# Attention with a gate beside it: first weights in halves, a regrouped lead, another bank for V's last tile, and a tile finished by VectorE

## The chip, the cores and the metric

One NeuronCore of one Trainium2 chip. The metric is the device time of one execution, in microseconds (us). TensorE (PE) multiplies matrices into eight PSUM banks of 128 x 512 f32; VectorE (DVE) and ScalarE (ACT) read PSUM, GpSimd (POOL) does not touch it here; SyncE (SP), ScalarE and GpSimd issue transfers. Every engine works through its own instructions in the order in which the program wrote them, and semaphores hold an instruction back until what it reads is there and what it overwrites has been used.

## The reference

x is 2048 x 512. The result mixes two branches, g a + (1 - g) b, with g = sigmoid(x . gate_w):

```python
qkv = (x @ wqkv).reshape(B, S, 3, 32, 16)            # 32 heads of 16
p = softmax(einsum("bhqd,bhkd->bhqk", q, k) * 16 ** -0.5)
a = einsum("bhqk,bhkd->bhqd", p, v) ... @ wo
r = x @ w_r;  idx = argsort(-r)[:2]                  # two routed tokens
y = (silu(x[idx] @ w_gate) * (x[idx] @ w_up)) @ w_down * sigmoid(r[idx])
b = x with y added in the rows idx
```

## The kernel before, in words

**Numbers in two pieces.** Projections are made of f32 split into a high and a low f32r piece (`split`, L68: ScalarE writes the high piece, VectorE or GpSimd the difference). A product then has three terms: high by high, high by low, low by high.

**Attention.** Heads are worked in pairs, a pair in two halves of 1024 queries: a unit. There are 32 units of 16 steps, one step for each tile of 128 keys. `s_piece` (L664) makes 128 keys x 512 queries of scores transposed (S) for one head and has ScalarE take the exponential into P (L674); the two heads lie in different rows of the array (partitions 0 and 64). `av_mm` (L689) multiplies P by V into the bank av over a unit's 16 steps; V carries a column of ones, which gives the sums. The exponentials need each query's largest score first. That is a second product of Q and K, 48 rows deep, reduced by VectorE (`m_piece`, L578): 64 products a unit, `EL`. When a unit's are there, `m_unit` (L640) combines them, and `m_rows` (L654) puts the negated maxima as two more rows below Q by eight small transfers, so that S comes out already lowered.

**The banks.** Tags of the PSUM pool: st (three banks, S and, at the beginning, projections and V), mxa (two banks as one tile), mxb, fl and av (one each). A tile waits until what was in its bank has been read.

**The order.** It is written out by hand (`manual_schedule`). First TensorE is kept busy with ten matmuls of zeros (L231). `load_w(0)` (L111) asks for the first projection weights, K's part first, and with them the first block of x: two of its four pieces by ScalarE's queue, all else by SyncE's. Projections of pair group 0 follow (`proj0`), evicted into split tiles that are stored to HBM and, for the first pair, copied straight into Kx and Qx.

Then comes the lead (L1000): `LEAD` = 21 steps, in which `m_lead` (L612) makes the maxima of the first unit and a part of the second ahead of any S, and `parts_next` mixes in the parts of `lead_parts` (L305): four parts of the last Q projection and 64 parts of V, a part being three matmuls (`v_part`, L294); four parts make one tile of V in an st bank. A lead step makes two pairs of maxima products, one pair into mxa and one into two of mxb, fl and av in turn, has three reductions of them, and then three parts (four in the first step). `end_step(s)` runs what is due after step s: `products` and `sums` (GpSimd multiplies x by w_r and by gate_w, ScalarE sums the rows), loads, `split_w(1)` after step -5, and after step -1 `r_row` (L342), which transposes the 2048 router scores on TensorE.

The main loop (L1009) follows `ORDER`, four steps a pass: s is an S piece, m a maxima product, A the P V of an earlier step, f a piece of other work (later projections, the routed feed-forward, the output projection). The first two A's have no P V to do yet; they take the parts of V that the lead has left over, two each.

**The tail** (L789) is what the last unit leaves: normalise its result and multiply it by wo for tiles 12 to 15 (L836), with the output products of tiles 9, 10 and 11 put between (`late_wo`). A tile of the output is finished either by `finish` (L560: one VectorE instruction reads PSUM, scales by g and adds to acc) or by `acc_add` (L474: ScalarE scales into a buffer, GpSimd adds it to acc). `store` (L564) writes a finished tile by SyncE's queue; tile 15 goes out in two halves by ScalarE's.

Of the kernel before, what the change touches and what calls it, by code (L numbers as in the profile page):

```python
# [21 lines left out]
KT = S // 128  # L22
VW = DH + 1
LEAD = 21
STEPS = UNITS * KT
EL = 64
# [10 lines left out]
def gated_mix(ctx: ExitStack, tc: tile.TileContext, xT, x, wqkv, wo, w_rg, w_gate, w_up, w_down,  # L37
# [18 lines left out]
    def mxa_tile():  # L56
        return psum.tile([128, 2, 512], F32, tag="mxa", name="mxa", bufs=1)
# [4 lines left out]
    def av_tile():  # L62
        return psum.tile([128, 512], F32, tag="av", name="av", bufs=1)
# [48 lines left out]
    def load_w(g):  # L112
        ws = ring.tile([128, 2, 4, 128], F32, tag="w", name="ws", bufs=3)
        W[g] = ws
        for i in (1, 0):
            if g == 0 and i == 0:
                load_x(0)
            nc.sync.dma_start(ws[:, i], ap(wqkv, (2 * g + i) * 128 * D, [[D, 128], [128, 4], [1, 128]]))

    def split_w(g, parts=(1, 0)):  # L120
# [14 lines left out]
    def load_x(nb):  # L135
        xst.append(ring.tile([128, 4, 512], F32, tag="xs" if nb < 2 else "P", name="xs", bufs=2 if nb < 2 else 3))
        for c in range(4):
            eng = nc.scalar if nb == 0 and c % 2 == 0 else nc.sync
            eng.dma_start(xst[nb][:, c], ap(xT, (nb * 4 + c) * 128 * 512, [[512, 128], [1, 512]]))

    def split_x(nb):
# [86 lines left out]
    warm = ring.tile([128, 512], mybir.dt.bfloat16, tag="o", name="warm", bufs=6)  # L228
    nc.vector.memset(warm, 0.0)
    wps = st_tile()  # L230
    for _ in range(10):  # L231
        nc.tensor.matmul(wps, warm[:, :128], warm, start=True, stop=True)
    load_w(0)
    for nb in range(1, 4):
# [58 lines left out]

    def v_part(t, c):  # L294
        if c == 0:
            VP[t] = st_tile()
        ps = VP[t]
        nb, tt = divmod(t, 4)
        sl = slice(tt * 128, tt * 128 + 128)
        for n, (a, b) in enumerate(((xh, wv[1]), (xl, wv[1]), (xh, wv[2]))):  # L300
            nc.tensor.matmul(ps, a[nb][:, c, sl], b[:, c, :], start=c == 0 and n == 0, stop=c == 3 and n == 2)  # L301
        if c == 3:
            nc.scalar.activation(Vh[:, t, :, :DH], ps.rearrange("p (h d) -> p h d", d=DH), AF.Copy)  # L303

    def lead_parts():  # L305

        v = [(t, c) for t in range(KT) for c in range(4)]
        yield from proj(0, "q", 3, 3)
        while v:
            v_part(*v.pop(0))  # L310
            yield


    rg = {}
# [27 lines left out]
    def r_row():  # L342
        ps = fl_tile((16, 128))
        nc.tensor.transpose(ps, gz[:, :, 0], ident)
        rg["row"] = ring.tile([16, 128], F32, tag="rt", name="rt", bufs=1)
        late.append((nc.scalar.activation, (rg["row"], ps, AF.Copy)))

    def route_rows():

# [124 lines left out]
    def acc_add(t, ps, scale):  # L474
        a = acc[t // 4][:, t % 4, :]
        w = o_tile("w", [128, D])
        nc.scalar.activation(w, ps, AF.Copy, scale=scale[:, t:t + 1])  # L477
        nc.gpsimd.tensor_add(a, a, w)  # L478
# [132 lines left out]

    def m_lead(n):  # L612

        if n < 16:
            u, t, c = 0, n // 8 * 4 + n % 4, n // 4 % 2 * 2
        else:
            u, t, c = 1, (n - 16) // 2, n % 2 * 2
        for i in range(3):
            if i == 0:
                tl = mxa_tile()  # L620
                dst = [tl[:, 0], tl[:, 1]]
            else:
                tl = (mxb_tile, fl_tile, av_tile)[(2 * n + i) % 3]()
                dst = [tl]
            for k, d in enumerate(dst):
                j, cc = (k, c) if i == 0 else (i - 1, c + 1)
                nc.tensor.matmul(d, Qx[u][64 * j:64 * j + 48, t * 128:t * 128 + 128],  # L627
                                 Kx[0][64 * j:64 * j + 48, cc * 512:cc * 512 + 512], start=True, stop=True)
            o = EL * u + t * 8 + (c * 2 if i == 0 else c * 2 + 1 + i)
            reds.append((Mr[:, o:o + len(dst)], tl))  # L630
        for r in reds:
            nc.vector.tensor_reduce(*r, axis=AX.X, op=OP.max, negate=True)  # L632
        reds.clear()
        if n == 15:
            m_unit(0)
        elif n == 16:
            m_rows(*turn.pop())

    reds = []
# [156 lines left out]
    def tail():  # L796
# [31 lines left out]
            sl = slice(256 * t, 256 * t + 256)  # L828
            split(hl[0][:, sl], hl[1][:, sl], o[:, sl])
        late_wo(2)  # L830
        acc_add(9, pw[2], gg)
        store(9)
        banks = [st_tile(), av_tile(), st_tile(), mxb_tile()]
        for t, n in ((0, 0), (0, 1), (1, 0), (1, 1), (0, 2), (1, 2), (2, 0), (2, 1), (2, 2), (3, 0), (3, 1), (3, 2)):
# [18 lines left out]
    def at_step(s, f, *a):  # L853
        fill.setdefault(s, []).append((f, a))

    def end_step(s):
        now[0] = s
        for f, a in fill.pop(s, []):
            f(*a)
# [130 lines left out]
    def parts_next(n):  # L990
        for _ in range(n):
            next(parts, None)
# [16 lines left out]
    while count["m"] < UNITS * EL:  # L1009
# [71 lines left out]
```

## Time and profile before

| | us |
|---|---|
| three runs: median, lowest, highest | 1415.55, 1415.53, 1415.92 |
| the profiled execution | 1415.73 |
| its span, first to last instruction | 1413.8 |
| TensorE busy in it | 1405.9 |
| VectorE, ScalarE, GpSimd busy | 1287.5, 1169.9, 316.7 |

The span is what the profile's clock counts from the first instruction on; 1.9 us of the execution lie around it. Times in rows are microseconds from the start of the span, and a row reads: start, length, engine, line of the kernel, operation, what it writes and reads, how many instructions; in square brackets stands how long the engine was idle before, and what ended that. Matmuls are pipelined: the length of a row of matmuls includes the fill, and the distance between starts says how fast they follow each other. The granted TensorE clock in the profile is 1.000.

### The profile page before, as it was taken

To read this page: it belongs to the slowest core of one execution; us is meant where nothing else is said; L and a number is where in the kernel's file an instruction comes from. 1 tells how busy PE (TensorE), PEld (TensorE's weight loads), DVE (VectorE), ACT (ScalarE), POOL (GpSimd) and SP (SyncE) were. 2 spreads that over 40 slices of the span, in tenths; PEclk is the share of its full clock that TensorE was granted. 3 is DMA by queue.
4 is the path that set the end of the run, shared out by engine and by line. 5 is a ranking of instruction groups with operands and counts; after the bars stand their busy time and mean duration, and the time that the engine had idled before them with its cause. 6 is when DMAs were issued, how large, how long until landed. Compare 5 with 4: busy or idle time off the path is not lost.

```text
span 1413.8 us, 24075 instructions
## 1 busy us (share of the span) xinstructions
PE 1405.9 (99%) x9109; PEld 626.4 (44%) x9109; DVE 1287.5 (91%) x1535; ACT 1169.9 (83%) x2263; POOL 316.7 (22%) x335
## 2 busy tenths in 40 slices
PE   9999999999999999999999999999999999999998
PEld 6654444444444444444444443344444444444433
DVE  6889999999999999999999999999999999999943
ACT  5568888888888888888888888888888888888986
POOL 3841101102000001200000100043722322224411
PEclk9999999999999999999999999999999999999999
DMA  8712111312123221312222342424312121111002
GB/s 265 272 31 57 46 40 39 84 39 69 44 74 101 70 61 39 83 38 72 66 91 61 93 102 76 103 60 120 84 46 54 32 68 29 29 31 51 15 32 99
DMA packets 54775, 101.24 MB, mean 72 GB/s; under 512 B 13168, under 2 KB 20592, under 8 KB 53028
## 3 DMA queue, kind: packets, MB, share of 16 engines
q1 hardware_dynamic: 53796, 98.62, 24.6%
q8 instruction: 72, 1.18, 0.4%
q10 hardware_dynamic: 576, 0.79, 0.2%
q0 software_dynamic: 288, 0.30, 0.1%
q14 instruction: 43, 0.35, 0.1%
HBM read 63.77 MB, written 36.96 MB: 71 GB/s over the span
## 4 chain that ended last, share of the span: by engine, by line
PE 99%; DMA 0%; ACT 0%; DVE 0%; issue 0%; DVEq 0%
PE av L695 36%; PE st L672 23%; PE mxa L592 12%; PE mxb L592 10%; PE fl L155 6%; PE fl L511 4%; PE st L301 3%; PE st L155 2%; PE mxa L627 1%; PE fl L402 1%; PE mxa L672 0%; PE fl L440 0%; DMA ws<-wqkv 0%; PE mxa L511 0%; PE fl L627 0%; PE mxb L627 0%
## 5 line engine op out<-in xcount | busy, mean ns | idle before, releaser
L674 ACT ACTIVATE P<-st 128x512 f32<-128x512 f32 x2009 | 1055.3, 599 | 188.5 <-PE st L672 101.7
L596 DVE TENSOR_REDUCE Mr<-mxa 128x2 f32<-128x1024 f32 x655 | 796.1, 1215 | 2.6 <-PE mxa L592 2.5
L695 PE MATMUL av<-P,V 128*32 128x512 f32 x4096 | 545.6, 605 | 0.2 <-DVE o L704 0.2
L672 PE MATMUL st<-Qx,Kx 50*128 50x512 f32 x2009 | 531.4, 443 | 0.8 <-ACT P L674 0.6
L596 DVE TENSOR_REDUCE Mr<-mxb 128x1 f32<-128x512 f32 x654 | 451.0, 690 | 61.0 <-PE st L672 18.8
L672 PEld LDWEIGHTS st<-Qx,Kx 50*128 50x128 f32 x2009 | 276.5, 184 | 228.3 <-ACT P L674 208.7
L592 PE MATMUL mxb<-Kx,Qx 48*128 48x512 f32 x654 | 325.2, 497 | 0.0
L592 PE MATMUL mxa<-Kx,Qx 48*128 48x512 f32 x1310 | 294.1, 417 | 0.0
L592 PEld LDWEIGHTS mxb<-Kx,Qx 48*128 48x128 f32 x654 | 119.5, 183 | 273.7 <-DVE Mr L596 272.8
L695 PEld LDWEIGHTS av<-P,V 128*32 128x32 f32 x4096 | 81.1, 108 | 142.7 <-issue 135.9
L592 PEld LDWEIGHTS mxa<-Kx,Qx 48*128 48x128 f32 x1310 | 123.1, 183 | 44.3 <-DVE Mr L596 2.6
L208 POOL TENSOR_SCALAR ev<-pe 128x512 fp32r<-128x512 f32 x24 | 35.8, 1490 | 411.5 <-ACT pe L206 411.5
L478 POOL TENSOR_TENSOR acc<-acc,w 128x512 f32<-128x512 f32 x36 | 46.1, 1280 | 201.0 <-ACT w L477 200.9
L77 POOL TENSOR_SCALAR hl<-m 128x16 fp32r<-128x16 f32 x31 | 7.8, 253 | 296.5 <-DVE m L643 296.5
L155 PE MATMUL fl<-xh,wh 128*128 128x512 f32 x96 | 42.9, 447 | 0.0
L155 PE MATMUL fl<-xh,wl 128*128 128x512 f32 x96 | 40.5, 422 | 0.0
L511 PE MATMUL fl<-woh,ahl 128*128 128x512 f32 x96 | 35.1, 447 | 0.0
L562 DVE SCALAR_TENSOR_TENSOR acc<-fl,gg,acc 128x512 f32<-128x512 f32 x11 | 8.2, 747 | 28.8 <-PE fl L511 28.8
L632 DVE TENSOR_REDUCE Mr<-mxa 128x2 f32<-128x1024 f32 x21 | 25.7, 1222 | 8.5 <-PE mxa L627 8.5
L155 PE MATMUL fl<-xl,wh 128*128 128x512 f32 x96 | 32.6, 421 | 0.0
L303 ACT ACTIVATE V<-st 128x512 f32<-128x512 f32 x16 | 9.6, 600 | 27.5 <-PE st L301 27.5
L209 POOL TENSOR_TENSOR ev<-pe,ev 128x512 fp32r<-128x512 f32 x24 | 30.8, 1285 | 2.0
(192 smaller groups left out, 786.4 us busy)
## 6 DMA issues: line engine op xcount, KB each, us to landing
Kx<-k_scr SPq DMA_DIRECT2D x30, 384.0 KB
Qx<-q_scr SPq DMA_DIRECT2D x52, 192.0 KB
q_scr<-ev SPq DMA_DIRECT2D x15, 512.0 KB
k_scr<-ev SPq DMA_DIRECT2D x13, 512.0 KB
xn<-x SPq DMA_DIRECT2D x4, 1024.0 KB
Qx<-hr SPq DMA_DIRECT2D x256, 2.0 KB
acc<-x_scr SPq DMA_DIRECT2D x4, 1024.0 KB
q_scr<-ev SPq DMA_DIRECT2D x15, 256.0 KB
```

The source lines that it names most:

```text
L155: nc.tensor.matmul(ps, a[:, i, c, :], b[nb][:, c, :], start=n == 0, stop=n == 11)
L208: nc.gpsimd.tensor_scalar(ev[:, 0], t, 1.0, None, op0=OP.mult)
L209: nc.gpsimd.tensor_sub(ev[:, 1], t, ev[:, 0].bitcast(F32))
L301: nc.tensor.matmul(ps, a[nb][:, c, sl], b[:, c, :], start=c == 0 and n == 0, stop=c == 3 and n == 2)
L478: nc.gpsimd.tensor_add(a, a, w)
L511: nc.tensor.matmul(ps, a[:, sl], b[:a.shape[0], c, :], start=first and n == 0, stop=last and n == 2)
L592: nc.tensor.matmul(dst, Qx[u % 3][64 * j:64 * j + 48, t * 128:t * 128 + 128], k_of(u, t // 4)[64 * j:64 * j + 48, c * 512:c * 512 + 512], ...
L596: nc.vector.tensor_reduce(Mr[:, g0:g0 + (2 if r == 1 else 1)], MX[r - 1], axis=AX.X, op=OP.max, negate=True)
L632: nc.vector.tensor_reduce(*r, axis=AX.X, op=OP.max, negate=True)
L672: nc.tensor.matmul(ps, k, q, start=True, stop=True)
L674: nc.scalar.activation(P[s][:, 2 * j + c, :], ps, AF.Exp)
L695: nc.tensor.matmul(AV[0][32 * ct:32 * ct + 32, :], V[:, kt, h * VW:h * VW + 32], P[s][:, ct, :], start=kt == 0, stop=kt == KT - 1)
```

## The change

Four edits.

1. The first weights (K's part) come in two halves of 128 KB, one by SyncE's queue and one by ScalarE's; of x's first block one piece instead of two then goes by ScalarE's queue, the second. Nine matmuls of zeros instead of ten.
2. The lead has 14 groups instead of 21 steps, each with three pairs of maxima products: one in mxa, one in an st bank and av, one in mxb and fl. The 84 products are the same in number. Five reductions a group; five parts after it, or four (in groups 1, 4, 7, 10 and 13), so 65 in all instead of 64. Two groups run the `end_step` of three steps, one after the first and two after the second. `m_unit(0)` comes after group 10, `m_rows` after group 11, `load_q(1)` before group 6.
3. V's last tile is made in the bank av instead of in st. `r_row` is no longer due after step -1 but is the last of `lead_parts`, behind V, and ScalarE's copy of its row is written at once instead of by the next `run_late`.
4. In the tail, tile 9 is finished by VectorE (`finish`) instead of by ScalarE and GpSimd (`acc_add`).

```diff
-            if g == 0 and i == 0:
+            if g == 0 and i == 1:
+                for e, eng in ((0, nc.sync), (2, nc.scalar)):
+                    eng.dma_start(ws[:, i, e:e + 2], ap(wqkv, 128 * D + e * 128, [[D, 128], [128, 2], [1, 128]]))
                 load_x(0)
+                continue
...
-            eng = nc.scalar if nb == 0 and c % 2 == 0 else nc.sync
+            eng = nc.scalar if nb == 0 and c == 1 else nc.sync
...
-    for _ in range(10):
+    for _ in range(9):
...
-            VP[t] = st_tile()
+            VP[t] = av_tile() if t == KT - 1 else st_tile()
...
             v_part(*v.pop(0))
             yield
+        r_row()
+        yield
...
-        late.append((nc.scalar.activation, (rg["row"], ps, AF.Copy)))
+        nc.scalar.activation(rg["row"], ps, AF.Copy)
...
     def m_lead(n):
-        if n < 16:
-            u, t, c = 0, n // 8 * 4 + n % 4, n // 4 % 2 * 2
-        else:
-            u, t, c = 1, (n - 16) // 2, n % 2 * 2
         for i in range(3):
+            p = 3 * n + i
+            if p < 32:
+                u, t, c = 0, p // 16 * 4 + p // 2 % 4, p // 8 % 2 * 2 + p % 2
+            else:
+                u, t, c = 1, (p - 32) // 4, p % 4
             if i == 0:
-                tl = mxa_tile()
-                dst = [tl[:, 0], tl[:, 1]]
+                tl = [mxa_tile()]
+                dst = [tl[0][:, 0], tl[0][:, 1]]
             else:
-                tl = (mxb_tile, fl_tile, av_tile)[(2 * n + i) % 3]()
-                dst = [tl]
-            for k, d in enumerate(dst):
-                j, cc = (k, c) if i == 0 else (i - 1, c + 1)
+                dst = tl = [st_tile(), av_tile()] if i == 1 else [mxb_tile(), fl_tile()]
+            for j, d in enumerate(dst):
                 nc.tensor.matmul(d, Qx[u][64 * j:64 * j + 48, t * 128:t * 128 + 128],
-                                 Kx[0][64 * j:64 * j + 48, cc * 512:cc * 512 + 512], start=True, stop=True)
+                                 Kx[0][64 * j:64 * j + 48, c * 512:c * 512 + 512], start=True, stop=True)
...
-        if n == 15:
+        if n == 10:
             m_unit(0)
-        elif n == 16:
+        elif n == 11:
             m_rows(*turn.pop())
...
-        acc_add(9, pw[2], gg)
+        finish(9, pw[2])
...
-    at_step(-1, r_row)
...
-    for s in range(-LEAD, 0):
-        now[0] = s
-        if s == -11:
+    for n in range(LEAD * 2 // 3):
+        now[0] = n * 3 // 2 - LEAD
+        if n == 6:
             load_q(1)
-        m_lead(s + LEAD)
-        parts_next(3 + (s == -LEAD))
-        end_step(s)
+        m_lead(n)
+        parts_next(4 if n % 3 == 1 else 5)
+        for s in range(n * 3 // 2, (n + 1) * 3 // 2):
+            end_step(s - LEAD)
```

More of the change, by code (lines that the diff above doesn't have):

```diff
@@ L612, in m_lead @@
     def m_lead(n):
-        if n < 16:
-            u, t, c = 0, n // 8 * 4 + n % 4, n // 4 % 2 * 2
-        else:
-            u, t, c = 1, (n - 16) // 2, n % 2 * 2
         for i in range(3):
+            p = 3 * n + i
[3 more added lines that the diff above has]
+                u, t, c = 1, (p - 32) // 4, p % 4
             if i == 0:
-                tl = mxa_tile()
-                dst = [tl[:, 0], tl[:, 1]]
-            else:
-                tl = (mxb_tile, fl_tile, av_tile)[(2 * n + i) % 3]()
-                dst = [tl]
-            for k, d in enumerate(dst):
-                j, cc = (k, c) if i == 0 else (i - 1, c + 1)
+                tl = [mxa_tile()]
+                dst = [tl[0][:, 0], tl[0][:, 1]]
+            else:
+                dst = tl = [st_tile(), av_tile()] if i == 1 else [mxb_tile(), fl_tile()]
+            for j, d in enumerate(dst):
                 nc.tensor.matmul(d, Qx[u][64 * j:64 * j + 48, t * 128:t * 128 + 128],
-                                 Kx[0][64 * j:64 * j + 48, cc * 512:cc * 512 + 512], start=True, stop=True)
-            o = EL * u + t * 8 + (c * 2 if i == 0 else c * 2 + 1 + i)
-            reds.append((Mr[:, o:o + len(dst)], tl))
+                                 Kx[0][64 * j:64 * j + 48, c * 512:c * 512 + 512], start=True, stop=True)
+            o = EL * u + t * 8 + c * 2
+            w = 2 // len(tl)
+            for j, k in enumerate(tl):
+                reds.append((Mr[:, o + j:o + j + w], k))
         for r in reds:
```

## The prediction

> **What bounds the kernel now.** I read the page first (busy time, then the chain that ended last), then a table of four stretches, then the instructions in order of time where the diff touches.
>
> ```profile
> span 1413.8 us, 24075 instructions
> PE 1405.9 (99%) x9109; PEld 626.4 (44%) x9109; DVE 1287.5 (91%) x1535; ACT 1169.9 (83%) x2263; POOL 316.7 (22%) x335
> PE 99%; DMA 0%; ACT 0%; DVE 0%; issue 0%; DVEq 0%
> ```
>
> The chain is TensorE from end to end, so a microsecond counts only if TensorE's sequence gets shorter, or waits less, or if the stores after its last instruction end sooner. The stretches (span from:to, length, then busy time of each engine) are the lead, the first pass of the main loop up to the first P V, the rest of the loop, and the tail:
>
> ```profile
> 25.20:87.80 62.60, 62.60 (x280) 41.06 (x279) 52.40 (x69) 30.65 (x83) 44.20 (x37) 1.00 0.59 196
> 87.80:97.38 9.58, 8.96 (x39) 4.72 (x38) 5.42 (x6) 6.42 (x14) 1.24 (x2) 1.00 0.00 1
> 97.38:1398.00 1300.62, 1300.21 (x8641) 557.52 (x8639) 1208.27 (x1424) 1110.72 (x2130) 256.88 (x280) 1.00 0.23 61
> 1398.00:1413.80 15.80, 10.80 (x65) 6.28 (x61) 6.38 (x13) 5.04 (x9) 2.57 (x2) 1.00 0.36 134
> ```
>
> The third stretch, 1300.62 us with 0.4 us of idle TensorE, isn't edited; what is gained or lost before 97.38 passes through it unchanged. The profiled execution took 1415.73 us, 0.18 over the median of 1415.55; I make the sum against it and carry the difference to the median.
>
> **Edit 1, the first weights in halves.** Rows of the chain, the timeline of ScalarE, and the DMA rate in slices of 0.2 us from 0 to 8 us:
>
> ```profile
> 0.74 3.64 DMA ws<-wqkv
> 5.61 19.68 PE st L155 x84
> ...
> 4.94 2.30 ACT L70 ACTIVATE xh<-xs 128x512 fp32r<-128x512 f32 x4
> ...
> GB/s 0 0 0 0 0 0 0 0 51 113 20 61 123 276 358 379 399 410 400 400 399 420 399 400 420 389 430 389 420 369 451 369 410 389 389 410 369 389 399 389
> ```
>
> The halves (128 KB on each queue) land sooner: weights and first x block, 512 KB, are through at 3.8 us by the slices, and the weights landed at 4.38, a lag of 0.6; the first 256 KB alone are through at 3.15, so the weights land near 3.8. But the first projection needs all four x blocks too, 1280 KB with the weights, which pass the slices at 5.8 whichever queue carries them, and land near 6.4. ScalarE starts its fourth x block at about 6.6 (four in 2.30 us from 4.94). So at most 0.2 us is there to win. I take 0: whatever TensorE wins ahead of 25 us it loses at the wait on VectorE shown next. The Trainium skill says the same in "DMA: Bandwidth & Descriptors", section "Issuing engines are not separate DMA queues": transfers begun on several engines interleave on the same 16 DMA engines, and only issue time is saved; by it, too, the edit gives 0, and the trace agrees (about 400 GB/s with one queue or two). The warm-up matmul less ends behind the same wait: 0; its risk is a rival below.
>
> **Edit 2, 14 groups of three pairs.** One lead step of before, TensorE and VectorE:
>
> ```profile
> 40.75 0.50 PE L627 MATMUL mxa<-Kx,Qx 48*128 48x512 f32 x2
> 41.09 0.39 PE L627 MATMUL mxb<-Kx,Qx 48*128 48x512 f32 x1
> 41.41 0.50 PE L301 MATMUL st<-Kx,xh 128*128 128x512 f32 x1
> 41.75 0.39 PE L301 MATMUL st<-Kx,xl 128*128 128x512 f32 x1
> ...
> 43.37 0.39 PE L301 MATMUL st<-wvl,xh 128*128 128x512 f32 x1
> 43.69 0.50 PE L627 MATMUL mxa<-Kx,Qx 48*128 48x512 f32 x2
> ...
> 41.29 1.22 DVE L632 TENSOR_REDUCE Mr<-mxa 128x2 f32<-128x1024 f32 x1 [0.49 <-PE mxa L627]
> 42.43 0.68 DVE L632 TENSOR_REDUCE Mr<-av 128x1 f32<-128x512 f32 x1
> 43.03 0.68 DVE L632 TENSOR_REDUCE Mr<-mxb 128x1 f32<-128x512 f32 x1
> ```
>
> A step is two pairs and nine projection matmuls, 2.94 us. Inside a run of one form starts lie 0.23 apart (41.75 to 43.37 is seven gaps); at the changes of form the gaps are 0.34, 0.32, 0.34 and 0.32 (40.75, 41.09, 41.41, 41.75; 43.37 to 43.69). A change and back thus costs 0.39 us over four plain gaps, and seven of 21 go: -2.7 us. "TensorEngine Tiling (Array Packing)", section "Key Properties", in the Trainium skill says that a change of tiling mode drains TensorE; it has no price, the rows have.
>
> Checked from the other side: before is 21 x 2.94 + 0.69 for the fourth part of the first step + 0.12 for the transposition of r = 62.55, against 87.80 - 25.22 = 62.58 in the trace (rows below). After, a group with five parts is 2.94 + 0.23 for the third pair + six matmuls of 0.23 = 4.55, one with four parts 3.86; nine and five of them give 60.25, and hold 65 parts instead of 64.
>
> VectorE per group: 1.14 + 4 x 0.60 = 3.54 (starts of the three rows above), below 3.86, so it keeps up, except at the beginning, where it starts late:
>
> ```profile
> 25.22 0.50 PE L627 MATMUL mxa<-Kx,Qx 48*128 48x512 f32 x2
> 26.14 0.60 ACT L73 ACTIVATE ev<-st 128x512 fp32r<-128x512 f32 x1 [2.94 <-DMA k_scr<-ev]
> 27.38 1.21 DVE L632 TENSOR_REDUCE Mr<-mxa 128x2 f32<-128x1024 f32 x1
> ```
>
> ScalarE's eviction waits for a store of K to free its buffer, and the subtraction and then the reductions stand behind it, until 27.38. Five reductions instead of three then hold the banks to 27.38 + 3.54 + 0.1 = 31.0; the second group's third pair is due at 25.22 + 4.55 + 0.57 = 30.34 and waits 0.7, with a restart 0.8. The next is due at 35.0 and gets its bank at 35.2: 0.3 with a restart. Bounds: 0 if the store lands 0.7 earlier, 2 if the third group is caught as deeply as the first. I take 1.08, so the lead is 61.33: first S matmul at 86.55, 1.25 us earlier than 87.80.
>
> The rows for the row-maximum DMAs (m_rows) move closer to that matmul:
>
> ```profile
> 76.15 5.39 SPq L663 DMA_DIRECT2D Qx<-hr  x8
> ```
>
> After, their transposition ends at about 78.0 (group 11 begins at 73.6, VectorE is through 4.4 later), the eight issues at 83.5, with 3 us left to land. No cost; cover 1.5 us or so.
>
> **Edit 3, V's last tile and r's row.** The first pass of the main loop, and what ScalarE and GpSimd do before it:
>
> ```profile
> 87.59 0.27 PE L344 MATMUL fl<-cst,gz 128*16 128x128 f32 x1
> 87.80 1.15 PE L672 MATMUL st<-Qx,Kx 50*128 50x512 f32 x3
> 91.05 0.40 PE L672 MATMUL st<-Qx,Kx 50*128 50x512 f32 x1
> 91.89 0.50 PE L672 MATMUL st<-Qx,Kx 50*128 50x512 f32 x1 [0.44 <-ACT P L674]
> 97.38 1.07 PE L695 MATMUL av<-P,V 128*32 128x512 f32 x8
> ...
> 78.47 2.55 POOL L71 TENSOR_TENSOR wl<-ws,wh 128x512 fp32r<-128x512 f32 x2 [2.21 <-ACT wh L70]
> 86.03 0.63 ACT L332 ACTIVATE p<-p 128x512 f32<-128x512 f32 x1 [0.53 <-POOL p L328]
> ```
>
> At the gaps above, this sequence without waits would take 7.65 us; it took 9.58, so 1.93 are waits, the largest at 91.89 (0.84 after its neighbour, not 0.23), because V's last tile holds one of S's three banks. After, three projection matmuls fewer stand here and r's transposition more (0.21 by 87.59 to 87.80): 7.19. The bank wait goes, and another comes. Two steps' sums now end the lead behind each other on ScalarE, and group 13's stand right before the first exponentials. The weight split (L71) waits for its ScalarE half until 80.6: group 11's parts end at 78.1 and finish a V tile, whose eviction takes ScalarE to 78.8; then come two sums of 0.6 and one ACTIVATE of 0.63. Six GpSimd instructions of 1.25 follow it, to 88.1; the last sums end at 88.9, against 86.7 before, and the exponentials queue behind them on ScalarE. S's fourth to sixth matmuls then wait about 0.4, 0.15 and 0.5. So 7.19 + 1.1 = 8.27, -1.31. Bounds: 2.4 gained if no wait is left, 0 if the sums run 1.3 later still. V's tile in av costs nothing: its bank is reduced third, about 3.0 after the group's start, and asked for at 3.2; P V asks for it 2 us after its eviction.
>
> **Edit 4, tile 9.** VectorE, GpSimd and the last stores, and the DMA rate from 1408 to 1414 in slices of 0.15 us:
>
> ```profile
> 1405.76 0.76 DVE L71 TENSOR_TENSOR onl<-o,onh 128x256 fp32r<-128x256 f32 x2 [0.16 <-ACT onh L70]
> 1406.72 1.30 POOL L478 TENSOR_TENSOR acc<-acc,w 128x512 f32<-128x512 f32 x1 [19.17 <-ACT w L477]
> 1407.24 0.75 DVE L562 SCALAR_TENSOR_TENSOR acc<-st,gg,acc 128x512 f32<-128x512 f32 x1 [0.72 <-PE st L836]
> 1408.05 1.82 SPq L565 DMA_DIRECT2D out<-acc  x4
> 1409.36 1.10 ACTq L848 DMA_DIRECT2D out<-acc  x2
> GB/s 0 0 0 0 0 68 314 396 382 437 314 355 437 410 328 369 396 382 341 376 328 375 369 437 314 382 355 328 341 198 7 0 0 0 0 0 0 0 0 0
> ```
>
> The chain shows VectorE here, but the stores set the end: 1.31 MB flow without a gap from 1408.8 to 1412.5, and SyncE's queue begins with tile 9, ready at 1408.02. VectorE has 0.72 idle before 1407.24, and the new instruction takes 0.75 of it: tile 12 is late by 0.03 at most. Tile 9 can leave at 1407.25. Tile 12 follows at 1408.0 as before and tile 14 at 1408.9, so gaps open, and the flow is dense again from about 1409.75 with 0.79 MB left, 2.2 us at 357 GB/s: an end at 1411.95, -0.6; with the 385 GB/s of its best slices, -0.7. Bounds 0 and 0.8; I take 0.65.
>
> **Sum:** 0 - 1.25 - 1.31 - 0.65 = -3.2; 1415.73 becomes 1412.5, and the median 1412.4.
>
> **Rivals.**
> (a) *Fewer waits than I count* in the lead's beginning and at the first exponentials: 1.1 us more, 1411.3. For it: the late start is one DMA's landing. Chance 0.10.
> (b) *The front at half rate.* The warm-up rows speak to it:
>
> ```profile
> 3.72 0.15 PEld L232 LDWEIGHTS <-warm 128*128 128x128 bf16 x1 [0.28 <-issue]
> 4.15 0.32 PEld L232 LDWEIGHTS <-warm 128*128 128x128 bf16 x2 [0.27 <-issue]
> ```
>
> They run 0.43 apart, then two within 0.32, at the end of the warm-up; the projection runs at 0.23. If nine don't bring the change of rate, some 3.8 us more run at 0.43: nine matmuls, 1.8 us lost, of which the wait on VectorE takes 0.9. That gives 1413.3. Against it: the rate changes before the ninth ends. Chance 0.10. "TensorE: Matmul & The Clock Gate", section "What's actually happening", in the Trainium skill has this as a gate that opens after a busy window and has a phase of its own.
> (c) *The stores end where they did*, because the last two issues of ScalarE at 1409.36 to 1410.46 set them, or the lead loses 0.7 more: 1413.1. Chance 0.12.
> (d) *Slower:* S's ring now carries maxima between V's tiles. If a group's second pair got the bank of the V tile just finished, it would wait for that eviction, which stands on ScalarE behind sums waiting for GpSimd (0.53 at 86.03). Some 1.0 a group over 13 groups is +13, about 1425; it decides from 0.46 a group, (3.2 + 2.8) / 13. Against it: a maximum's bank is released in program order ahead of V's, so it is handed out first. Chance 0.08.
>
> **How the numbers follow.** A measurement of this kernel tells about 0.2%, 2.83 us, from no change: the line is 1412.7. The forecast has 0.60 (its own range 1411.7 to 1413.1), of it 0.13 above that line. Faster: 0.47 + 0.10 = 0.57; within: 0.13 + 0.10 + 0.12 = 0.35; slower 0.08. The range goes from 1411.0, past (a), to 1414.2, past (b) and (c).
>
> **What would show it.** Front: wh of ScalarE near 3.8, the first projection matmul still at 5.6 to 5.7. Lead: 14 groups of 4.55 and 3.86, two waits on VectorE's fl before 36 us, first S near 86.5. First pass: L301 into av, S waiting for ACT at the fourth to sixth matmul, first P V near 94.8. Tail: no GpSimd for tile 9, its store near 1404.7 on the shifted clock, stores ending 0.65 closer to the last TensorE instruction. Wrong would make it: V or S waiting for a bank in every group, or rows of the projection 0.43 apart after 5.6 us.

## The result

The changed kernel takes 1413.07 us in the median against 1415.59 for the kernel before: a ratio of 0.9982, 95% interval 0.9976 to 0.9988, or 2.5 us less. Its single runs spread more than the old kernel's: 1412.0 to 1413.9 instead of 1415.2 to 1416.4. One slow run of 2409.64 us, of which there is no trace, is left out of that range. The prediction said 1412.4. The profiled execution took 1412.45 us, with a span of 1410.6, so the median lies 0.6 above the execution that the trace shows; that gap is part of the story.

The first view is the table of stretches of the changed kernel, cut at the same four places as in the prediction: lead, first pass, rest of the loop, tail. Its columns are from:to, length, and busy time of each engine.

```profile
25.68:86.30 60.62, 60.62 (x280) 42.85 (x279) 52.75 (x76) 29.89 (x79) 42.96 (x37) 1.00 0.57 192
86.30:94.45 8.15, 8.15 (x37) 4.34 (x36) 5.86 (x7) 7.32 (x18) 2.19 (x3) 1.00 0.29 76
94.45:1394.83 1300.38, 1299.99 (x8640) 557.70 (x8639) 1208.53 (x1424) 1110.18 (x2129) 257.17 (x280) 1.00 0.23 61
1394.83:1410.60 15.77, 10.80 (x65) 6.28 (x61) 7.04 (x14) 4.45 (x8) 1.27 (x1) 0.99 0.36 134
```

| stretch | before | after | difference | predicted |
|---|---|---|---|---|
| up to the first maxima product | 25.20 | 25.68 | +0.48 | 0 |
| lead | 62.60 | 60.62 | -1.98 | -1.25 |
| first pass | 9.58 | 8.15 | -1.43 | -1.31 |
| rest of the loop | 1300.62 | 1300.38 | -0.24 | 0 |
| tail | 15.80 | 15.77 | -0.03 | -0.65 |
| sum | 1413.80 | 1410.60 | -3.20 | -3.21 |

The sum fits almost exactly, and two of its terms don't: the front loses half a microsecond, and the tail gains nothing. The lead makes up for them. That the fit is this close is luck: from the first P V to the start of the last TensorE instruction, where no edit changes TensorE's work, the traced executions (those without a fall of the clock there) took anything from 1309.97 to 1311.03 us.

**The front.** ScalarE, then TensorE, in the changed kernel's timeline:

```profile
3.44 1.28 ACT L70 ACT_TABLE_LOAD   x1 [3.44 <-DMA ws<-wqkv]
4.74 0.63 ACT L70 ACTIVATE wh<-ws 128x512 fp32r<-128x512 f32 x1
5.94 0.50 PE L158 MATMUL st<-xh,wh 128*128 128x512 f32 x1 [1.25 <-ACT xh L70]
7.10 0.63 ACT L70 ACTIVATE xh<-xs 128x512 fp32r<-128x512 f32 x1 [0.17 <-DMA xs<-xT]
```

The first half of the weights is there at 3.44; the whole came at 4.38 before. But ScalarE's table load, 1.28 us, now begins only when that half has landed (in the kernel before it ran at 1.66, ahead of the wait for them), and the high piece is made at 4.74 instead of 4.40. The projection starts at 5.94 instead of 5.61, and ScalarE gets the fourth piece of x only at 7.10.

**The lead.** Starts of the groups and of the late products on TensorE:

```profile
25.68 0.50 PE L631 MATMUL mxa<-Kx,Qx 48*128 48x512 f32 x2
...
30.20 0.50 PE L631 MATMUL mxa<-Kx,Qx 48*128 48x512 f32 x2
...
34.06 0.50 PE L631 MATMUL mxa<-Kx,Qx 48*128 48x512 f32 x2
...
34.81 0.50 PE L631 MATMUL fl<-Kx,Qx 48*128 48x512 f32 x1
...
38.87 0.50 PE L631 MATMUL mxa<-Kx,Qx 48*128 48x512 f32 x2
...
77.46 0.50 PE L631 MATMUL mxa<-Kx,Qx 48*128 48x512 f32 x2
...
78.35 0.50 PE L631 MATMUL fl<-Kx,Qx 48*128 48x512 f32 x1
...
82.40 0.51 PE L631 MATMUL mxa<-Kx,Qx 48*128 48x512 f32 x2
```

VectorE's first reduction, and the subtraction in `m_unit`, with that of the kernel before (L648) last:

```profile
27.03 1.22 DVE L638 TENSOR_REDUCE Mr<-mxa 128x2 f32<-128x1024 f32 x1
...
73.55 1.21 DVE L654 TENSOR_TENSOR hl<-m,hl 128x16 fp32r<-128x16 f32 x1
...
73.46 0.18 DVE L648 TENSOR_TENSOR hl<-m,hl 128x16 fp32r<-128x16 f32 x1
```

A group with five parts takes 4.52 (25.68 to 30.20) and one with four 3.86 (30.20 to 34.06), as predicted. Two groups are longer. In the third the fl product stands 0.75 after the group's start, not 0.58 as in the first, and the group takes 4.81, 0.29 over 4.52: that is the second of the two predicted waits on fl, and the first, priced at 0.8, is gone. In the thirteenth it stands 0.89 after the start, and the group takes 4.94, 0.42 over: ahead of it the subtraction of 128 x 16 numbers took VectorE 1.21 us, a term that the prediction doesn't have. The waits at the beginning are thus 0.29, not 1.08. The lead as a whole lies 60.62 - 60.25 = 0.37 over the sum without waits, less than 0.29 + 0.42, because the groups without a wait are a little shorter than priced.

**The first pass.** S's fourth to sixth matmuls, the maxima product beside the sixth, and ScalarE's exponentials, in the changed kernel:

```profile
88.81 0.49 PE L678 MATMUL st<-Qx,Kx 50*128 50x512 f32 x1
...
89.30 0.98 PE L678 MATMUL st<-Qx,Kx 50*128 50x512 f32 x2
89.79 0.73 PE L597 MATMUL mxa<-Kx,Qx 48*128 48x512 f32 x2
...
88.18 3.01 ACT L680 ACTIVATE P<-st 128x512 f32<-128x512 f32 x6
```

V's last tile holds none of S's banks any more. The last sums end at 88.28, and the exponentials queue behind them, as forecast. S's fifth and sixth matmuls come 0.49 after their neighbours instead of 0.23, and so wait about 0.25 each; the profile puts the idle time before their weight loads (0.30 each) down to ScalarE's exponentials. The fourth, for which 0.4 was forecast, comes 0.34 after a product of V, the usual gap at a change of form. The rest of the 8.15 - 7.19 = 0.96 us of waits, some 0.45, lies later in the pass.

### The profile page after: what moved, and what is told of

Same layout as the page of the kernel before. It is cut to its first block, busy times and chain, and to the rows that moved or that the text cites. A ratio compares the mean times of both kernels' runs of the same rounds, so it can differ in the third digit from the quotient of the medians.

```text
span 1410.6 us, 24079 instructions
## 1 busy us (share of the span) xinstructions
PE 1402.7 (99%) x9108; PEld 627.8 (45%) x9108; DVE 1289.5 (91%) x1543; ACT 1169.0 (83%) x2262; POOL 315.4 (22%) x334
## 4 chain that ended last, share of the span: by engine, by line
PE 99%; DMA 0%; DVE 0%; ACT 0%; SPq 0%; issue 0%; DVEq 0%
PE av L701 36%; PE st L678 23%; PE mxa L597 12%; PE mxb L597 10%; PE fl L158 6%; PE fl L516 4%; PE st L304 3%; PE st L158 1%; PE fl L407 1%; PE mxa L631 0%; DMA xs<-xT 0%; PE mxa L678 0%; PE fl L445 0%; PE st L631 0%; PE av L304 0%; PE mxb L631 0%
## 5 line engine op out<-in xcount | busy, mean ns | idle before, releaser
L601 DVE TENSOR_REDUCE Mr<-mxa 128x2 f32<-128x1024 f32 x655 | 796.4, 1216 | 1.4 <-PE mxa L597 1.3
L477 POOL TENSOR_SCALAR acc<-acc,omg 128x512 f32<-128x512 f32 x16 | 24.8, 1562 | 11.4 <-DMA acc<-x_scr 11.4
```

Of the source, the lines that this page charges most:

```text
L477: nc.gpsimd.tensor_scalar(a, a, omg[:, t:t + 1], None, op0=OP.mult)
L601: nc.vector.tensor_reduce(Mr[:, g0:g0 + (2 if r == 1 else 1)], MX[r - 1], axis=AX.X, op=OP.max, negate=True)
```

## The experiments

Each series ran beside the kernel before on the same chip; differences are between medians of that series. All kernels compute the whole result.

| kernel | median | lowest to highest | against before |
|---|---|---|---|
| changed kernel | 1413.07 | 1412.01 to 1413.88 | -2.52 |
| edit 1 alone | 1416.81 | 1415.29 to 1417.43 | +1.64 |
| edit 4 alone | 1414.48 | 1414.19 to 1414.96 | -0.69 |
| one DMA more | 1415.45 | 1415.18 to 1415.60, one 1418.42 | +0.28 |
| without edit 1 | 1411.36 | 1410.94 to 1412.39 | -3.81 |
| before, nine matmuls of zeros | 1415.08 | 1414.84 to 1416.71 | +0.08 |
| changed, eleven matmuls of zeros | 1411.82 | 1411.35 to 1412.20 | -3.18 |
| changed, table load first | 1412.07 | 1411.15 to 1413.04 | -2.93 |
| edit 2 alone | 1419.63 | 1414.07 to 1421.95 | +4.63 |
| edit 2, V's last tile in av | 1412.23 | 1411.71 to 1414.12 | -3.29 |
| without edit 1, eleven zeros, earlier weight split | 1417.05 | 1410.95 to 1421.38 | +1.53 |
| without edit 1, eleven zeros | 1411.18 | 1411.08 to 1411.53 | -3.85 |

### Edit 1: what the halves and the ninth matmul cost

Without edit 1, in the changed kernel (and the same lines, the other way round, for edit 1 alone):

```diff
-            if g == 0 and i == 1:
-                for e, eng in ((0, nc.sync), (2, nc.scalar)):
-                    eng.dma_start(ws[:, i, e:e + 2], ...)
+            if g == 0 and i == 0:
                 load_x(0)
-                continue
...
-            eng = nc.scalar if nb == 0 and c == 1 else nc.sync
+            eng = nc.scalar if nb == 0 and c % 2 == 0 else nc.sync
...
-    for _ in range(9):
+    for _ in range(10):
```

> The changed kernel without edit 1 (edits 2 to 4 stay). Theory: edit 1 costs time in two places. At the front the first projection matmul comes at 5.94 with it and at 5.61 without, and the fourth x piece is there at 7.08 instead of 6.47; at the end the one DMA more puts the last store of tile 15 on a semaphore that SyncE checks first instead of last. So without it: first projection matmul near 5.6, first maxima product near 25.2 instead of 25.68 (half of which VectorE's late start eats in the first two groups), the last of SyncE's final waits shorter, and 0.4 to 0.8 us less than the changed kernel: 1412.3 to 1412.7 where that has 1413.07. Rival, as predicted: the halves cost nothing, the difference is within 0.2 us.

> The kernel before with edit 1 alone. Theory: slower by 0.4 to 0.9 us (some 0.4 at SyncE's final waits, 0 to 0.5 of the front that the wait on VectorE in the lead doesn't swallow): 1416.0 to 1416.5 against 1415.6. Rival, as predicted: 0, the projection still starts at 5.6 and what is won or lost ahead of 25 us is lost or won at VectorE's late start.

Without edit 1: 1411.36 against 1415.17, ratio 0.9976 (0.9966 to 0.9985), 3.8 us. Edit 1 alone: ratio 1.0010 (1.0001 to 1.0019), 1.64 us slower, which is twice what I expected, and its eleven runs lie in two groups: five from 1415.3 to 1416.0 and six from 1416.8 to 1417.4. The profiled execution belongs to the lower one; no trace of the upper one was taken. Waits at the front explain 0.3 to 0.5 of it, not a second group some 1.5 above the first. So edit 1 costs, and "0" falls, but not by the theory alone.

The next two kernels change the number of matmuls of zeros and nothing else: nine in the kernel before, eleven in the changed kernel.

```diff
# the kernel before
-    for _ in range(10):
+    for _ in range(9):
# the changed kernel
-    for _ in range(9):
+    for _ in range(11):
```

> The kernel before with nine matmuls of zeros instead of ten, and nothing else. Edit 1 alone cost 1.64 us in the median, with single runs in two groups (1415.3 to 1416.0 and 1416.8 to 1417.4); the profiled executions show the change of TensorE's rate anywhere from 4.0 us on, in one of them only after the tenth matmul of zeros. Theory of the short warm-up (rival (b) of the prediction): nine end near 5.0, and where the rate hasn't changed by then it changes late, in a part of the runs: two groups here too, the upper one 1 to 1.8 us above the lower, median 0 to 1.5 above the kernel before. Rival: the spread comes with the halves (table load and x pieces late); then this kernel is as the one before, one group, within 0.2.

> The changed kernel with eleven matmuls of zeros instead of nine: at half rate they end at 1.18 + 11 x 0.43 = 5.9, where the first projection matmul starts. Theory of the short warm-up: the upper group of runs (1413.5 to 1413.9) disappears, the median falls by 0.6 to 0.9 to some 1412.2, the lower group (1412.0 to 1412.7) stays. Rival, spread from the halves' transfers: both groups stay, the median as the changed kernel's, 1413.07 less what the chip differs.

Both came out as the theory of the short warm-up has it. With nine, seven runs of the old kernel stay at 1414.8 to 1415.2 and four go to 1416.3 to 1416.7. This time the profiled execution (1416.61) is of the upper group, and TensorE's timeline shows it:

```profile
5.85 0.80 PE L155 MATMUL st<-xh,wh 128*128 128x512 f32 x1 [0.64 <-ACT xh L70]
6.45 0.63 PE L155 MATMUL st<-xh,wl 128*128 128x512 f32 x1
6.87 0.63 PE L155 MATMUL st<-xh,wh 128*128 128x512 f32 x1
...
10.84 0.39 PE L155 MATMUL st<-xh,wh 128*128 128x512 f32 x1
11.06 0.39 PE L155 MATMUL st<-xh,wl 128*128 128x512 f32 x1
...
27.25 0.50 PE L627 MATMUL mxa<-Kx,Qx 48*128 48x512 f32 x2
```

The projections follow each other by 0.43 us until 10.84, and by 0.23 from there: twelve matmuls at half rate. The granted clock reads 1.00 from 0 to 12 us all the same, so only the spacing shows this rate. From the first projection to the first maxima product it takes 21.40 us instead of the 19.61 of the kernel before, 1.79 more, and that product is at 27.25 instead of 25.22. Little of it is swallowed: the first S comes at 89.66, 1.86 after that of the kernel before, and the upper group lies 1.6 above the lower. In the changed kernel eleven matmuls gave one group, 1411.35 to 1412.20, 3.18 under the kernel before instead of 2.52: the upper part of its runs (seven from 1413.5 to 1413.9) is gone.

Where is the rest of edit 1's cost? The same kernel with eleven matmuls takes -3.18 with the halves and -3.85 without them, two series whose intervals overlap. Two suspects were tried. The first is the table load, made early by an ACTIVATE that waits for no transfer:

```diff
+    z = ring.tile([128, 1], F32, tag="rt", name="z", bufs=1)
+    nc.vector.memset(z, 0.0)
+    nc.scalar.activation(z, z, AF.Copy)
```

> The changed kernel with a one-column ACTIVATE of a constant tile written right behind the first loads, so that ScalarE's table load (1.28 us) no longer stands behind the wait for the weights (3.44 to 4.72 in the changed kernel, 1.66 to 2.94 before). Theory that the table load holds the front: the high piece of the weights at about 3.8 instead of 4.74, the first projection matmul at 5.0 to 5.4 instead of 5.94. What is left of it behind the wait for the fourth x piece (landed at 7.08) and behind VectorE's late start: 0.1 to 0.4 us in the median. Rival: the x pieces set the front whatever ScalarE does, first maxima product still near 25.7, 0.

ScalarE's timeline of that kernel:

```profile
1.66 1.28 ACT L239 ACT_TABLE_LOAD   x1 [1.66 <-PEq L1083]
...
3.71 0.63 ACT L70 ACTIVATE wh<-ws 128x512 fp32r<-128x512 f32 x1 [0.56 <-DMA ws<-wqkv]
...
6.95 0.63 ACT L70 ACTIVATE xh<-xs 128x512 fp32r<-128x512 f32 x1 [0.43 <-DMA xs<-xT]
```

The high piece of the weights is now at 3.71, the projection at 5.48. But the fourth piece of x still comes only at 6.95, and the first maxima product moves from 25.68 to 25.55: 0.13 us. The rival named the binding thing. In the median the kernel lies 0.4 lower, which its interval (0.9969 to 0.9987 against 0.9976 to 0.9988) doesn't settle, with the runs as spread as before. Its profiled run (1412.55) is no low one, though its projections are 0.23 apart from the start. VectorE's timeline, TensorE's second and third group and the stretch of the lead show why:

```profile
27.87 1.21 DVE L641 TENSOR_REDUCE Mr<-mxa 128x2 f32<-128x1024 f32 x1
...
30.07 0.50 PE L634 MATMUL mxa<-Kx,Qx 48*128 48x512 f32 x2
...
34.93 0.50 PE L634 MATMUL mxa<-Kx,Qx 48*128 48x512 f32 x2
```

```profile
25.55:87.15 61.60, 61.40 (x280) 43.02 (x280) 52.73 (x76) 29.68 (x79) 42.97 (x37) 1.00 0.58 191
```

VectorE's first reduction came at 27.87 instead of 27.03, the second group took 4.86 us instead of 3.86, and the lead 61.60 instead of 60.62. So the spread has at least two causes, as far as these single executions show: the rate and VectorE's start.

The second suspect is the end of the kernel. SyncE's last instructions wait for all transfers, one semaphore after the other (eleven semaphore instructions of SyncE stand there in the trace). If the transfers take their semaphores in turn, then the one DMA that edit 1 adds puts every later one on the next semaphore. No view shows that assignment. The experiment adds one DMA in the middle of the kernel before:

```diff
-        nc.sync.dma_start(x_scr[i * 512:i * 512 + 512, :], x[i * 512:i * 512 + 512, :])
+        for r in ((0, 256), (256, 512)) if i == 0 else ((0, 512),):
+            nc.sync.dma_start(x_scr[i * 512 + r[0]:i * 512 + r[1], :], x[i * 512 + r[0]:i * 512 + r[1], :])
```

> The kernel before with one copy in the middle of the kernel (x to its scratch, first block) split into two DMAs of half the size; the work and the front are unchanged. Theory of the order of the final waits: one DMA more shifts every later DMA to the next of eight semaphores, the last store then sits on the one that SyncE checks first, and eight checks of some 0.06 us come behind it instead of none: 0.4 us slower, 1416.0, with the last TensorE instruction unmoved. Rival: the order of the waits costs nothing, 0 within 0.15.

Two views each of before, of after, and of one DMA more: SyncE's waits at the end (us in total, times, longest), and the DMA rate over the last 6 us of the span in slices of 0.15 us.

```profile
SPq L1077 <- DMA out<-acc: 2.6, 5, 0.7
```

```profile
GB/s 0 0 0 0 0 0 0 287 369 355 423 396 342 355 437 382 328 341 437 396 341 321 382 355 348 437 355 382 308 335 301 27 0 0 0 0 0 0 0 0
```

```profile
SPq L1083 <- DMA out<-acc: 2.5, 1, 2.5
```

```profile
GB/s 0 82 369 355 382 410 151 273 355 382 382 328 28 232 382 355 410 355 321 355 383 348 437 369 376 301 335 267 21 0 0 0 0 0 0 0 0 0 0 0
```

```profile
SPq L1078 <- DMA out<-acc: 2.9, 1, 2.9
```

```profile
GB/s 0 0 0 0 273 396 314 423 382 355 369 423 410 328 341 410 423 341 328 355 355 382 417 376 341 321 355 280 41 0 0 0 0 0 0 0 0 0 0 0
```

Before, SyncE waits five times for stores, and eight empty slices (1.2 us) lie behind the last transfer. With one DMA more it waits once, and eleven empty slices, 1.65, follow: that is 0.45 us, in the changed kernel too. It fits the theory, by which the one wait is for the last store and the other semaphores are still to be checked behind it. The median gives +0.28, with an interval of 0.9995 to 1.0013 that holds no change. The traces are more regular than the medians: from the start of the last TensorE instruction to the end of the span it is 5.39 us before, 5.82 with one DMA more, 5.80 with edit 1 alone, 4.90 with edit 4 alone, 4.92 without edit 1, and 5.36 in the changed kernel. So the one DMA costs 0.43, and edit 4 wins 0.49.

With this most of the cost of the halves is found: of the 0.67 between the kernels with eleven matmuls, their traces show 0.38 behind the start of the last TensorE instruction (5.30 and 4.92) and 0.14 at the first P V (94.45 and 94.31).

### Edit 4 alone

```diff
-        acc_add(9, pw[2], gg)
+        finish(9, pw[2])
```

> The kernel before with edit 4 alone (tile 9 finished by VectorE). The prediction says 0.65 less, from denser stores; the trace of the changed kernel shows the last landing 0.49 closer to the last TensorE instruction. Without edit 1's extra DMA nothing takes that away at the final waits, so 0.5 less is expected: 1415.1. Rival: the issues of ScalarE's last two stores set the end and nothing is won.

It won 0.69 in the median, with one group of runs, 1414.2 to 1415.0, where the prediction had 0.65; the interval (0.9985 to 1.0003) just holds no change, and the trace shows 0.49, as said above. In the changed kernel edit 4 wins this too, and the DMA more takes 0.43 of it back.

### Edits 2 and 3: the lead, V's last tile and r's row

Edit 2 alone is the kernel before with the new `m_lead` and its loop, V's last tile in st and `at_step(-1, r_row)` kept. The second is one more execution of the same kernel, with its trace.

> The kernel before with edit 2 alone (the lead in 14 groups, old front, V's last tile in st, r's row after step -1). The prediction: seven changes of form less, -2.7, one part of V more in the lead (+0.69, which the first pass gives back), waits for VectorE in the first two groups +1.08 (traces of the changed kernel without edit 1 show some 0.5): 1.6 to 2.3 us less in sum. Rival (d): maxima in st's ring wait for V's evictions in every group, slower than before. Rival: the gain is in edit 3 and little of it here, under 1 us. With all but edit 1 having gained 3.81 and edit 4 alone 0.69, edit 3's share is 3.1 less what this gains.

> A second look at edit 2 alone, whose eleven runs lay between 1414.1 and 1422.0 while the profiled one was the fastest. In that fast one the transposition of r's row waits 1.2 us for the last sums of ScalarE right before the first S matmul (86.80) and S waits for ScalarE at 88.65 and 92.10. What is to be seen is where a run of some 1417 to 1420 spends the rest. Theory of the first pass: the lead and its beginning as in the fast one (first maxima 25.4, first S near 87), the loss at the first S and exponentials and what follows them. Theory of the front: the rate of TensorE changes late, projections 0.43 apart, first maxima 1 to 2 us later. Theory (d): waits of 0.5 and more for V's evictions in most groups of the lead, first S beyond 90.

Alone, edit 2 is 4.6 us slower (ratio 1.0025, 1.0015 to 1.0036), where 1.6 to 2.3 less was expected, though its fastest run is 0.9 faster than the median of before. Here are two executions of it, first the one of 1414.07, then the one of 1421.31; of each TensorE's timeline at the first S, and then rows of the table of stretches (after the busy times of five engines comes the granted clock):

```profile
86.80 0.28 PE L344 MATMUL fl<-cst,gz 128*16 128x128 f32 x1 [0.78 <-ACT p L332]
87.01 0.70 PE L673 MATMUL st<-Qx,Kx 50*128 50x512 f32 x2
88.65 0.50 PE L673 MATMUL st<-Qx,Kx 50*128 50x512 f32 x1 [0.94 <-ACT P L675]
```

```profile
85.00:91.00 6.00, 4.28 (x19) 2.40 (x17) 2.49 (x4) 4.13 (x11) 2.21 (x2) 1.00 0.57 145
91.00:103.00 12.00, 11.53 (x67) 5.16 (x68) 10.16 (x15) 9.27 (x19) 4.22 (x5) 1.00 0.00 1
```

```profile
87.81 0.28 PE L344 MATMUL fl<-cst,gz 128*16 128x128 f32 x1 [0.78 <-ACT p L332]
88.02 0.70 PE L673 MATMUL st<-Qx,Kx 50*128 50x512 f32 x2
89.66 0.49 PE L673 MATMUL st<-Qx,Kx 50*128 50x512 f32 x1 [0.94 <-ACT P L675]
...
90.91 0.63 PE L301 MATMUL st<-wvl,xh 128*128 128x512 f32 x1
```

```profile
85.00:91.00 6.00, 4.28 (x18) 2.65 (x18) 2.83 (x5) 4.61 (x13) 3.22 (x3) 0.99 0.64 153
91.00:103.00 12.00, 11.74 (x37) 5.58 (x35) 6.05 (x7) 5.53 (x11) 3.71 (x3) 0.50 0.00 1
103.00:106.00 3.00, 3.00 (x22) 0.86 (x14) 1.85 (x4) 1.27 (x3) 0.15 (x1) 0.75 0.00 0
```

Both have the same two waits: r's transposition waits for ScalarE's last sums, and S for a bank. In the second execution TensorE then runs at half rate from 90.9 to about 104, and does 37 matmuls in 12 us instead of 67. By the granted clock that is 12 x 0.5 + 3 x 0.25 = 6.75 us; from the first S to the last matmul it took 1325.99 us (88.02 to 1414.01), the other 1319.85 (87.01 to 1406.86), 6.1 less. So most of the loss lies where the first theory put it, at the first S and behind; the 1.0 us ahead of it is VectorE's late start, with the first reduction 2.47 behind the first maxima product instead of 1.34. The lead has no wait in every group, which is what (d) asked for. But the waits at the first S are the same in the execution of 1414.07. What differs is whether the clock falls, and why it falls in one and not in the other isn't shown. The runs without a trace go with it: the mean granted clock is 0.993 to 0.995 in the six from 1419.6 up, and 0.999 to 1.000 in the other five. What the three of these at 1415.9 to 1417.1 lost stays open.

Half of edit 3 added to edit 2:

```diff
-            VP[t] = st_tile()
+            VP[t] = av_tile() if t == KT - 1 else st_tile()
```

> Edits 2 and the first half of edit 3 (V's last tile in the bank av), r's row still right after step -1. Theory that V's last tile in S's ring makes edit 2 alone slow: the spread goes, about 1413.0 to 1413.5 (edits 2 and 3 without 1 and 4 come to about 1412.1 by the difference of the runs so far), the wait of r's row (some 1.2 us) stays. Theory that r's row makes it slow (TensorE waits for the last sums, and its copy stands before the exponentials): as edit 2 alone, spread to 1420.

With V's last tile in av: 3.29 us faster than before (0.9969 to 0.9987), one group but for a run of 1414.12. That was better than I expected. r's row still waits 0.71 there for the last sums, at 86.72, and the lead takes 61.64; the first pass takes 7.35 instead of 8.15. In that single trace the wait has moved across the first S, no more: moving r's row is worth nothing that can be measured (-3.29 and edit 4's -0.69 make -3.98, with r's row moved it is -3.81).

### Two versions that should be better

The first loads and splits the second weights earlier, so that GpSimd's chain ends sooner and the first exponentials don't stand behind the last sums:

```diff
-    at_step(-8, load_w, 1)
-    at_step(-5, split_w, 1)
+    at_step(-13, load_w, 1)
+    at_step(-9, split_w, 1)
```

> The changed kernel without the halves, with eleven matmuls of zeros, and with the second weights loaded at step -13 and split after step -9 instead of -8 and -5, so that GpSimd's chain, and with it the last sums ahead of the first exponentials, ends earlier. Without edit 1 alone the kernel was 3.8 us faster than before, in two groups of runs (1411.0 to 1411.5 and 1412.1 to 1412.4). Theory: eleven matmuls take away the upper group, and the earlier split takes 0.5 to 0.9 of the 0.96 us of waits in the first pass (8.12 against 7.19 without waits): 4.3 to 5 us faster than before, first P V near 93.2. Rival: the weights' copy slows ScalarE's and VectorE's evictions earlier in the lead, and nothing is won: 3.8.

> The changed kernel without the halves of the first weights and with eleven matmuls of zeros (edits 2 to 4 as they are, the second weights split where they were). Without edit 1 but with ten the runs lay in two groups, 1410.9 to 1411.5 and 1412.1 to 1412.4, median 3.8 us under the kernel before; with edit 1 and eleven one group, 3.2 under it. Theory that TensorE's late change of rate makes the upper group: eleven end at 5.9 at half rate, 0.3 after the first projection could start, but leave no room for the late change; one group, 3.6 to 4.2 us faster than before. Rival: the upper group has another cause (VectorE's late start, the first pass), then it stays and the median with it at 3.8 or 0.3 worse.

The first missed: three of twelve runs at 1411.0 to 1411.6, the others 1416.4 to 1421.4. Rows of VectorE and TensorE of its profiled execution (1418.76), and of its table of stretches:

```profile
74.29 4.77 DVE L651 TENSOR_TENSOR hl<-m,hl 128x16 fp32r<-128x16 f32 x1
...
80.25 0.50 PE L628 MATMUL mxa<-Kx,Qx 48*128 48x512 f32 x2 [1.99 <-DVE Mr L635]
...
82.00:89.00 7.00, 6.96 (x15) 4.93 (x16) 4.20 (x7) 0.11 (x1) 2.58 (x3) 0.52 0.02 2
```

and of GpSimd:

```profile
74.02 1.28 POOL L330 TENSOR_TENSOR p<-xn,wr 128x512 f32<-128x512 f32 x1
...
77.77 1.26 POOL L330 TENSOR_TENSOR p<-xn,wg 128x512 f32<-128x512 f32 x1
79.58 1.27 POOL L330 TENSOR_TENSOR p<-xn,wr 128x512 f32<-128x512 f32 x1 [0.56 <-ACT p L334]
```

The subtraction of 128 x 16 numbers took VectorE 4.77 us. It ended at 79.06, when GpSimd's four products without a gap between them ended at 79.03. In the changed kernel it took 1.21 and ended at 74.76, where one GpSimd product had ended at 74.73 and the next began; in the kernel before it took 0.18, with GpSimd idle. The earlier split had moved GpSimd's chain onto it. The reductions came late, TensorE stood 2 us, and the clock fell to 0.52 for 7 us. The nine upper runs have a mean granted clock of 0.996 to 0.998, the three lower ones 0.999 to 1.000.

The second version gives one group of runs, 1411.08 to 1411.53, 3.85 us faster than before (ratio 0.9972, 0.9961 to 0.9983). The changed kernel's ratio is 0.9982; the intervals overlap a little, the groups of runs, each taken against its own before (-3.95 to -3.5 here, -3.6 to -1.7 there), hardly. The upper group that the kernel without edit 1 had with ten matmuls (1412.1 to 1412.4) is gone; that a late change of rate made it is likely, but no trace of a run of that group was taken.

## Why the prediction was right, and where it was not

The time lay in the range, 0.7 over the forecast. The mechanism of edits 2 to 4 held; that edit 1 costs nothing did not. That the sum of the profiled execution was met to 0.01 us is luck: +0.48 at the front and +0.62 at the tail are cancelled by -0.73 in the lead, -0.12 in the first pass and -0.24 in a loop that varies by 1 us. The median lies 0.6 above that execution because of a spread that the sum has no term for.

- **Edit 1, "I take 0": wrong, in both of its reasons.** The landings were sized about right (the first half at 3.44, both by 3.71 in the run with the table load first; predicted 3.8). What I didn't see is that the table load on ScalarE can come behind a wait: in the kernel before it ran at 1.66, hidden, and I had no row for it; with the halves it ran only at 3.44. The first projection was at 5.94, not 5.6 to 5.7; I put the last piece of x at 6.4, and ScalarE got it at 7.10. Nor did the wait on VectorE swallow the loss.
- **Rival (b), chance 0.10: it happens, in a part of the runs.** Its price of 1.8 was met (1.79 in the traced run with nine matmuls of zeros); that 0.9 of it would be swallowed was wrong: four runs in eleven lay some 1.6 us higher. What failed is the step "the rate changes before the ninth ends": it rested on one execution, and I read the time of the change as a property of the kernel. With the halves, where TensorE stands idle longer before the projection (until 5.94), six of eleven runs were in the upper group; that the idle time is the reason isn't shown. The page "TensorE: Matmul & The Clock Gate" in the Trainium skill says in "What's actually happening" that the window is free-running and doesn't start with the kernel; the traces agree, with a change at about 4.2 in the kernel before and at 10.8 in that one with nine.
- **Edit 2: the mechanism and its unit price were right** (groups of 4.52 and 3.86 for 4.55 and 3.86). The mis-sized term is "I take 1.08" for the waits at the beginning: 0.29. The rule behind it holds: when the first reduction was 1.35 us behind the first maxima product (27.03 and 25.68), one group was 0.29 longer; when it was 2.32 behind (27.87 and 25.55), the second group alone was 1.00 longer. I had taken the delay of the kernel before, 2.16, as fixed. That is rival (a)'s "one DMA's landing", and it varies from run to run: 1.34 and 2.47 in two executions of edit 2 alone. So the half of rival (a) that is in the lead came true in the profiled execution, hidden by the losses at the front and the tail.
- **Edit 3: right in size (-1.43 for -1.31)**, and S waited for ScalarE at two of the three matmuls I named. I had priced the waits it removes at their length. Edit 2 without it shows that more is at stake: with those waits the clock fell in some executions, and then they cost 6 us more.
- **Rival (d)** did not come in the lead's groups; the slower outcome was there, though, one edit away, and by another mechanism.
- **Edit 4: near enough by itself (-0.69 in the median, -0.49 in the trace, for -0.65)**; in the whole kernel the DMA that edit 1 adds took 0.43 back behind the last store, a term I didn't have. So the outcome of rival (c), no gain at the end, came about by a cause that I hadn't named. m_rows cost nothing, as said.

## What to carry to other kernels

Price a wait of TensorE not only by its length: two waits of about 0.9 us close together cost nothing more in one execution and six in another, and the kernel with one of them removed lost the spread too. One trace shows one phase of the clock; when an edit touches the warm-up or opens a gap near it, take several runs and look for groups before believing the trace. Before moving a small VectorE instruction or a GpSimd chain, look which of them overlap in time, and count what the first ACTIVATE drags behind its waits.

## What the runs showed of the hardware

- The granted clock of TensorE fell in the middle of the kernel after 1.7 us of idle time in 6 us (4.28 busy from 85 to 91 in both executions of edit 2 alone), in one and not in the other, and stayed at half for about 13 us. At the front, matmuls at half rate (0.43 us apart until 10.84) stand beside a granted clock of 1.00.
- A VectorE subtraction with both inputs in SBUF took 0.18, 1.21 and 4.77 us for the same 128 x 16: short with GpSimd idle, and otherwise until a GpSimd product ended. The Trainium skill, "SBUF — State Buffer", section "Who interferes with whom", has VectorE instructions with two SBUF inputs contend with GpSimd instructions that read SBUF, by a port pair that is an exclusive lock; the 1.21 us agree with it, and the 4.77 us show more, no turn between four GpSimd instructions that follow each other.
- With one DMA more in the program, 1.65 us instead of 1.2 lie between the last transfer and the end of the span. That this is the last store's place in the order in which SyncE checks its semaphores is the theory that fits.
